# Retnet attention into a SwiGLU block on one core: the last quad of w_out's sums on VectorE, and ScalarE's part of the second tile's ticks at once

## The chip, the cores and the metric

One core of one Trainium2 chip runs the whole program in one launch. The metric is the device time of an execution in microseconds. The kernel before was run four times, and one more execution was profiled.

## What is computed

```python
# q, k, v: (8, 8, 576, 64); w_gate, w_val: (512, 1536); w_out: (1536, 512)
scores = scale * q @ k.T                       # for each batch and head, scale = 1/sqrt(64)
ret    = scores * D                            # D[i, j] = gamma_h ** (i - j) for i >= j, else 0
attn   = ret @ v
x      = attn.transpose(0, 2, 1, 3).reshape(4608, 512)
g      = x @ w_gate
out    = (g * sigmoid(g) * (x @ w_val)) @ w_out
```

All of it is float32.

## The kernel before

**Attention** runs over 32 *items*: 8 batches by 4 pairs of heads (HP = 4), numbered `i`. A pair's 576 tokens are cut into 9 chunks of 64. Within a chunk the masked scores are multiplied out; what earlier chunks give comes from a running state of 64x64 a head. `tick(t)` (L595) advances three items by one stage each: TensorE's values of item t-2 (L481 `own_values`, L500 to L504 `earlier_values`), the new states of item t-1 (L490) and its scores (L511 for the last chunk, L517). The work of the other engines in the tick is a list of *pieces* that `go_on` (L633) issues one or more at a time: `copies` (L528, `even`), `keys` (L459 and the like, the scaling of kn), `outputs` (`to_x`, L554 to L577, which write x), `own` (L524, `ret`), `states` (L532 `ret_last`, L534 to L539 `state`), the transposes of item t to qT and kT (L454), and last the load of item t+2. A load (L258) of an item from 4 on is 13 DMAs: eight of q and k (L291), two of kn and two of v (L272), one of `vl` (L301). They stand on SP's queue, except item 11's, which stand on ScalarE's. There are two buffers for q and k together, so a load waits until the transposes have read the buffer that it overwrites. For items that are `light` (L420, from 12 to 19) `keys`, the scaling of q and `outputs` are ScalarE's; else VectorE does most of it.

**The weights** arrive as bits of 64-bit numbers. `split` (L369, ScalarE, L378 and L379) and `rounding` (L384, VectorE) turn each half into float32; each rounding issues the next split.

**The first tile** of 512 tokens is multiplied plainly: `up0` (L645, L650), `down0` (L660, 12 down products of four matmuls in the order `down_order`), `out0` (L665), which copies the result and issues four output DMAs on ScalarE's queue (L670).

**Every further tile** has 1024 tokens and goes by a bilinear scheme: four by four blocks with 26 products instead of 32, for each of three quads of the up weights (`up_step` L854, matmuls L870, 78 in a tile) and once for all three quads of w_out (`down_step` L900, matmuls L909, 26 in a tile). A product's operands are sums of blocks, and its result is added into several parts (`reads` L797: copies L807 on ScalarE, sums L810 on VectorE or GpSimd). The weights' operands are made once and kept in DRAM: those of the up weights by `first_sums` and `w_sums` (L843, L830) during the second tile's up products, those of w_out by `out_sums` (L702) during the first tile. `fetch` (L766, L771) brings them back on SP's queue into a ring of 8 places, one fetch issued behind each product; the first eight, dn0 to dn7, are issued behind the last four products of the second tile's up phase.

**w_out's sums.** A list `OUT_SUMS` (L106) says, for each of 26 operands, which sums lead to it. `out_sums(qd)` makes nine groups of up to three operands of it for each quad. In `do` (L724) a sum takes the first free place of `sum_places` (six of 128x256, L693; 12 more, L694, from late in the first tile's up products on), and a finished operand is sent to DRAM (L728). A place goes back to the end of the list when its value is used no more; a sum that takes it again waits for the DMA that read it. `add` (L676) issues a sum on a given engine: L686 adds or subtracts, L679 and L684 negate, L681 is VectorE's one-instruction form of a negated sum that GpSimd makes with L683 and L684. Before the change all three quads are GpSimd's, and their DMAs SP's.

**Order.** The order on every engine is written by hand: the program order holds. Startup is L936 to L948; the first tile's up products and ticks 4 to 9 follow a plan (L957 to L986); in the loop L988 to L999 each down product of the first tile is followed by pieces of ticks 10 to 13, by `first_sums` and x's sums at its end, and by one or two of the groups of w_out's sums that are left. L1008 to L1027 are the tiles, in which ticks are spread over the products: `up_step` issues one piece behind each product, `down_step` three.

Of the kernel before, what the change touches and what calls it, by code (L numbers as in the profile page):

```python
# [17 lines left out]
ALU = mybir.AluOpType  # L18
# [136 lines left out]
def kernel(  # L155
# [32 lines left out]
    nc = tc.nc  # L188
# [331 lines left out]
    def masked(i):  # L520
        p, sr, (ret, ret_last, state) = i % HP, last_scores(i), places(i)

        def own():
            nc.vector.tensor_tensor(out=ret, in0=sc, in1=near[:, 2 * p : 2 * p + 2].unsqueeze(2).to_broadcast([P, 2, NFULL, L]),  # L524
                                    op=ALU.mult)

        def copies():
            (nc.vector.tensor_copy if vector(i + 1) else nc.scalar.copy)(out=even, in_=z[:, 0])  # L528

        def states():  # L530

            nc.vector.tensor_tensor(out=ret_last, in0=sr, in1=last_near[:, p], op=ALU.mult)  # L532
            at = state[:, 1:].rearrange("p (c r) d -> p c r d", r=2)[:, :, 1]
            nc.vector.scalar_tensor_tensor(out=at, in0=even, scalar=step[:, p : p + 1], in1=z[:, 1], op0=ALU.mult, op1=ALU.add)  # L534
            for c in range(1, NFULL):
                nc.vector.scalar_tensor_tensor(out=at[:, c], in0=at[:, c - 1], scalar=step[:, HP + p : HP + p + 1],
                                               in1=at[:, c], op0=ALU.mult, op1=ALU.add)
            at = state[:, 0 : NC - 1].rearrange("p (c r) d -> p c r d", r=2)
            nc.vector.scalar_tensor_tensor(out=at[:, :, 1], in0=at[:, :, 0], scalar=step[:, p : p + 1], in1=even,  # L539
                                           op0=ALU.mult, op1=ALU.add)  # L540

        return [copies, own, states]

# [51 lines left out]
    def tick(t, lo=HP, hi=NP, spread=False, then=None):  # L595
        go_on(len(pieces))
        if hi == HP:

            if lo <= t - 1 < hi:
                scores(t - 1, True)  # L600
                new_states(t - 1)
                for f in masked(t - 1):
                    f()
            if lo <= t - 2 < hi:
                own_values(t - 2)
                earlier_values(t - 2)
                to_x(t - 2)[0]()
            for f in transposes(t) if lo <= t < hi else ():
                f()
            return  # L610
        if lo <= t - 2 < hi:
            own_values(t - 2)
        if lo <= t - 1 < hi:
            new_states(t - 1)
        if lo <= t - 2 < hi:
            earlier_values(t - 2)
        if lo <= t - 1 < hi:
            scores(t - 1, t - 2 < lo)
        copies, *masks = masked(t - 1) if lo <= t - 1 < hi else (lambda: None,)
        keys, *new = transposes(t) if lo <= t < hi else (lambda: None,)  # L620
        outputs = to_x(t - 2)[0] if lo <= t - 2 < hi else lambda: None
        if t - 2 >= 0 and light(t - 2):
            pieces.append(lambda: (copies(), keys(), outputs()))
        else:
            pieces.extend([lambda: (copies(), keys()), outputs])
        pieces.extend(masks)
        pieces.extend(new)
        if then:
            pieces.append(then)
        if not spread:  # L630
            go_on(len(pieces))
# [33 lines left out]
    def out0():  # L665
        for i, bank in enumerate(banks):
            o = rest[:, part_at + 512 * i : part_at + 512 * (i + 1)]
            (nc.vector.tensor_copy if i > 1 else nc.scalar.copy)(out=o, in_=bank)
        for i in range(4):
            nc.scalar.dma_start(out=out[i * P : (i + 1) * P, :], in_=rest[:, part_at + 512 * i : part_at + 512 * (i + 1)])  # L670
# [5 lines left out]
    def add(eng, op, view, to=None):  # L676
        dst, srcs = view(int(op[1])) if to is None else to, [view(int(a)) for a in op[2:]]
        if op[0] == "neg":
            eng.tensor_scalar(out=dst, in0=srcs[0], scalar1=-1.0, scalar2=None, op0=ALU.mult)  # L679
        elif op[0] == "nad" and eng is nc.vector:  # L680
            eng.scalar_tensor_tensor(out=dst, in0=srcs[0], scalar=-1.0, in1=srcs[1], op0=ALU.mult, op1=ALU.subtract)  # L681
        elif op[0] == "nad":
            eng.tensor_tensor(out=dst, in0=srcs[0], in1=srcs[1], op=ALU.add)  # L683
            eng.tensor_scalar(out=dst, in0=dst, scalar1=-1.0, scalar2=None, op0=ALU.mult)  # L684
        else:
            eng.tensor_tensor(out=dst, in0=srcs[0], in1=srcs[1], op=ALU.add if op[0] == "add" else ALU.subtract)  # L686
# [3 lines left out]

    sum_places = [rest[:, sum_at + TB * i : sum_at + TB * (i + 1)] for i in range(6)]  # L693
    more_places = [rest[:, raw_at + TB * i : raw_at + TB * (i + 1)] for i in range(16) if i % 4]  # L694

    events = []
    for line in OUT_SUMS:
# [3 lines left out]

    def out_sums(qd):  # L702

        place = {}

        def view(s):
            return w_dn[:, qd, s // 2, s % 2] if s < 8 else place[s]

        def used(e):
            return [e[1]] if e[0] is None else [int(a) for a in e[1][2:]]  # L710

        def release(k):

            for s in list(place):
                for e in events[k + 1 :]:
                    if s in used(e):
                        break
                    if s == e[0]:
                        sum_places.append(place.pop(s))
                        break  # L720
                else:
                    sum_places.append(place.pop(s))

        def do(k):  # L724
            e = events[k]
            if e[0] is None:
                _, slot, i = e
                nc.sync.dma_start(out=dn_ops[i][:, qd * TB : (qd + 1) * TB], in_=view(slot))  # L728
            else:
                new = sum_places.pop(0)  # L730
                add(nc.gpsimd, e[1], view, new)
                if e[0] in place:
                    sum_places.append(place[e[0]])
                place[e[0]] = new
            release(k)

        r, ends = [], [k for k, e in enumerate(events) if e[0] is None]
        for g in range(0, N, 3):
            lo, hi = ends[g - 1] + 1 if g else 0, ends[min(g + 2, N - 1)] + 1

            def group(lo=lo, hi=hi):
                for k in range(lo, hi):
                    do(k)

            r.append(group)
        return r
# [188 lines left out]

    for t in range(HP + 2):  # L936
        tick(t, 0, HP)
        if t == 2:
            split(0)

        for j in {2: (0,), 3: (1, 2), 4: (3, 4, 5)}.get(t, ()):
            rounding(j)
        if t == 3:
            load(HP)
        if t > 3:
            for f in range(2):
                up0(f, range(2) if t == 4 else range(2, HP))
# [6 lines left out]
        if t + AHEAD < NP:  # L954
            load(t + AHEAD)

    groups = [(qd, group) for qd in range(NQ) for group in out_sums(qd)]  # L957
    todo = [m for m in range(3, len(order))]
    plan = []

# [7 lines left out]
    for f in range(2, NF):  # L968
        round_until({4: 12, 6: 13, 8: 14, 9: 15, 10: 16, 11: 17}.get(f, f + 2))
        plan.append(lambda f=f: up0(f, range(HP)))  # L970
        if f - 1 in tick_at and f < NF - 1:
            plan.append(lambda t=tick_at[f - 1]: next_load(t))
        if f in tick_at:
            plan.append(lambda t=tick_at[f]: tick(t, HP, FIRST))
        if f >= NF - 2:

            plan.append(lambda t=tick_at[f]: next_load(t))
        for _ in range(0 if f == 9 else 3):
            if f >= (7, 10, NF)[groups[0][0]]:
                if f + 1 == NF and more_places:  # L980
                    plan.append(lambda places=more_places[:]: sum_places.extend(places))
                    more_places.clear()
                plan.append(lambda group=groups.pop(0)[1]: group())
    assert not todo
# [3 lines left out]
    for m, f in enumerate(down_order):  # L988
        down0(f)
        go_on(4)  # L990
        if m in tick_at:
            tick(tick_at[m], HP, FIRST, tick_at[m] + 1 < needed(1))
            go_on(1)
        if m == 8:
            first_sums(0, 0, 4)
        if m > 8:
            x_sums(1, 3 * (m - 9), min(3 * (m - 8), X_FIRST), True)
        for _ in range(min(1 if m < 3 else 2, len(groups))):
            groups.pop(0)[1]()  # L999
    out0()  # L1000
    x_sums(1, X_FIRST, X_FIRST_OF_ALL, True)
    done = FIRST
# [55 lines left out]
```

## Time and profile before

| | before |
|---|---|
| four runs, us | 1081.28, 1083.24, 1088.47, 1078.66 |
| median, us | 1082.26 |
| profiled execution: its own time, us | 1080.27 |
| profiled execution: span on the core, us | 1078.6 |
| mean granted clock of TensorE | 0.989 |
| DVE busy in the span, us | 652.8 |
| POOL busy in the span, us | 414.4 |

Times in the trace count from the span's start. PE is TensorE, PEld its weight loads, DVE VectorE, ACT ScalarE, POOL GpSimd, SP SyncE; ACTq and SPq are the DMA issues on those engines' queues. In the timeline a row gives the start, the time from the first start to the last end of a run of like instructions, the engine, the line, the operation with its tiles (output <- inputs), how many there are, and in brackets the idle time of the engine before it with what ended it. In the list of waits a row gives the instruction that waited, what it waited for, us in total, how many times, and the longest. The granted clock is the share of full speed that TensorE was given.

The places that the change touches lie thus in the trace before: startup until 33 us, the first tile's up products until 128, its down products from 131.3 to 183.7 with ticks 10 to 13 at 138.4, 148.2, 161.4 and 171.2, the second tile's up products from 183.66 and its down products from 355.56.

### The profile page before, as it was taken

How to read it: one execution, taken by the hardware profiler on the slowest of the kernel's cores; microseconds unless marked ns; L12 is line 12 of the kernel's file. 1: busy time of each engine (PE TensorE's matmuls, PEld its weight loads, DVE VectorE, ACT ScalarE, POOL GpSimd, SP SyncE). 2: the span in 40 equal slices, each digit the busy share in tenths (PEclk: the TensorE clock that was granted, in tenths of full speed). 3: DMA queues.
4: the chain of work that ended last, by engine and by line, in shares of the span. 5: the costliest groups of instructions: out<-in, count | busy, mean ns of one | idle time of the engine just before them, and what ended most of it. 6: DMA issues, size and time to landing. Idle time of an engine off the chain costs nothing.

```text
span 1078.6 us, 21481 instructions
## 1 busy us (share of the span) xinstructions
PE 1042.8 (97%) x8420; PEld 855.1 (79%) x8420; DVE 652.8 (61%) x1069; ACT 271.6 (25%) x578; POOL 414.4 (38%) x372
## 2 busy tenths in 40 slices
PE   5999999699999999999999999999999999999998
PEld 4545555488788788888888888888888888888887
DVE  3568755577878857753647868536267455244644
ACT  3456400124333211222222112132221012231110
POOL 5002449666464403741216025622150374122505
PEclk9899999699999999999999999999999999999999
DMA  9798774766586868767657778554454555555653
GB/s 246 220 273 233 214 176 151 215 183 187 160 211 182 253 154 244 216 179 198 157 160 219 179 206 229 151 153 137 154 174 152 160 179 150 155 152 157 187 160 98
DMA packets 300700, 198.58 MB, mean 184 GB/s; under 512 B 215352, under 2 KB 244056, under 8 KB 300600
## 3 DMA queue, kind: packets, MB, share of 16 engines
q1 hardware_dynamic: 268230, 159.16, 54.2%
q10 hardware_dynamic: 31954, 37.17, 10.3%
q8 instruction: 67, 1.10, 0.4%
q0 software_dynamic: 416, 0.89, 0.2%
q14 instruction: 33, 0.27, 0.1%
HBM read 157.04 MB, written 40.11 MB: 183 GB/s over the span
## 4 chain that ended last, share of the span: by engine, by line
PE 80%; DVE 6%; POOL 5%; DMA 4%; issue 2%; SPq 1%; ACT 1%; ACTq 0%; DVEq 0%; POOLq 0%
PE bankC L870 11%; PE bankA L870 11%; PE bankB L870 11%; PE bankE L870 11%; PE bankA L909 6%; PE bankE L909 6%; PE bankB L909 6%; PE bankC L909 6%; POOL rest L686 3%; DVE rest L810 2%; PE bankA L650 2%; PE bankC L650 2%; PE bankB L650 2%; PE bankE L650 2%; PE outer L504 2%
## 5 line engine op out<-in xcount | busy, mean ns | idle before, releaser
L810 POOL TENSOR_TENSOR rest<-rest 128x512 f32<-128x512 f32 x56 | 79.2, 1419 | 298.6 <-DVE rest L810 278.0
L885 ACT ACTIVATE io<-rest 128x256 f32<-128x256 f32 x180 | 75.0, 417 | 342.9 <-DVE rest L810 296.4
L870 PE MATMUL bankA<-rest,arena 128*128 128x256 f32 x544 | 130.8, 384 | 4.5 <-ACT rest L807 3.6
L870 PE MATMUL bankC<-rest,arena 128*128 128x256 f32 x544 | 129.1, 380 | 0.5 <-DVE rest L810 0.5
L686 POOL TENSOR_TENSOR arena<-arena 128x512 f32<-128x512 f32 (+1 forms) x72 | 115.2, 1612 | 27.9 <-DMA up<-arena 20.1
L870 PE MATMUL bankE<-rest,arena 128*128 128x256 f32 x512 | 122.4, 382 | 0.8 <-DVE rest L810 0.8
L870 PE MATMUL bankB<-rest,arena 128*128 128x256 f32 x512 | 121.4, 380 | 0.4 <-DVE rest L810 0.4
L686 POOL TENSOR_TENSOR rest<-rest 128x256 f32<-128x256 f32 (+1 forms) x86 | 80.5, 958 | 105.7 <-issue 63.2
L870 PEld LDWEIGHTS bankA<-rest,arena 128*128 128x128 f32 x544 | 103.9, 192 | 20.7 <-issue 5.6
L892 POOL TENSOR_TENSOR arena<-rest,io 128x256 f32<-128x256 f32 x72 | 51.8, 726 | 167.1 <-ACT io L885 167.1
L870 PEld LDWEIGHTS bankC<-rest,arena 128*128 128x128 f32 x544 | 102.9, 190 | 15.3 <-issue 1.2
L870 PEld LDWEIGHTS bankE<-rest,arena 128*128 128x128 f32 x512 | 97.8, 192 | 14.8 <-issue 1.2
L870 PEld LDWEIGHTS bankB<-rest,arena 128*128 128x128 f32 x512 | 97.0, 190 | 14.3 <-DVE rest L810 0.8
L810 DVE TENSOR_TENSOR rest<-bankB,rest 128x512 f32<-128x512 f32 x72 | 48.9, 687 | 65.0 <-PE bankB L870 47.0
L810 DVE TENSOR_TENSOR rest<-bankE,rest 128x512 f32<-128x512 f32 x72 | 48.8, 686 | 64.3 <-PE bankE L870 45.8
L810 DVE TENSOR_TENSOR rest<-bankC,rest 128x512 f32<-128x512 f32 x72 | 48.8, 686 | 63.3 <-PE bankC L870 43.7
L810 DVE TENSOR_TENSOR rest<-bankA,rest 128x512 f32<-128x512 f32 x72 | 48.8, 685 | 61.4 <-PE bankA L870 43.0
L888 DVE SCALAR_TENSOR_TENSOR arena<-rest,io 128x256 f32<-128x256 f32 x84 | 58.7, 703 | 11.7 <-ACT io L885 11.7
L909 PE MATMUL bankA<-arena 128*128 128x256 f32 x252 | 58.0, 380 | 1.3 <-DVE arena L686 1.3
L909 PE MATMUL bankB<-arena 128*128 128x256 f32 x252 | 58.3, 381 | 0.0
L909 PE MATMUL bankC<-arena 128*128 128x256 f32 x252 | 58.1, 380 | 0.0
L909 PE MATMUL bankE<-arena 128*128 128x256 f32 x252 | 57.9, 379 | 0.0
(179 smaller groups left out, 1632.0 us busy)
## 6 DMA issues: line engine op xcount, KB each, us to landing
arena<-up SPq DMA_DIRECT2D x234, 256.0 KB
arena<-dn SPq DMA_DIRECT2D x104, 384.0 KB
up<-arena ACTq DMA_DIRECT2D x78, 256.0 KB
dn<-rest SPq DMA_DIRECT2D x78, 128.0 KB
out_dram<-rest SPq DMA_DIRECT2D x32, 256.0 KB
qk<-in_q_dram SPq DMA_DIRECT2D x108, 72.0 KB
qk<-in_k_dram SPq DMA_DIRECT2D x108, 72.0 KB
v<-in_v_dram SPq DMA_DIRECT2D x58, 128.0 KB
```

Of the source, the lines that this page charges most:

```text
L504: nc.tensor.matmul(xr[half[hl]] if c + 1 == NC else xo[half[hl ^ c % 2 * exchange(i)], c // 2, c % 2], state[half[hl], c, :], s["qT"][half ...
L650: nc.tensor.matmul(bank, w_up[:, f // 4, gv, f % 4, c // 2, (c % 2) * P : (c % 2 + 1) * P], xs[0][:, c, :], start=(c == 0), stop=(c == HP ...
L686: eng.tensor_tensor(out=dst, in0=srcs[0], in1=srcs[1], op=ALU.add if op[0] == "add" else ALU.subtract)
L810: eng.tensor_tensor(out=at(op[1]), in0=at(op[2]), in1=at(op[3]), op=ALU.add if op[0] == "add" else ALU.subtract)
L870: nc.tensor.matmul(b[:, gv * TB : (gv + 1) * TB], w[:, gv, ts(c, P)], rhs[:, c, :], start=(opens and gv == 0 and c == 0), stop=(c == 1), s ...
L885: nc.scalar.activation(out=s, in_=src[:, 0:TB], func=AF.Silu, scale=-1.0 if negative else 1.0)
L888: return lambda: nc.vector.scalar_tensor_tensor(out=dst, in0=src[:, TB : 2 * TB], scalar=-1.0, in1=s, op0=ALU.mult, op1=ALU.mult)
L892: nc.gpsimd.tensor_tensor(out=dst, in0=src[:, TB : 2 * TB], in1=s, op=ALU.mult)
L909: nc.tensor.matmul(b[:, m * TB : (m + 1) * TB], lhs[:, qd, ts(m, P)], w[:, qd], start=(opens and qd == 0 and m == 0), stop=(qd == NQ - 1), ...
```

## The change

It has three parts.

1. *Startup:* `split(0)` and `rounding(0)` are issued within tick 3, behind item 2's masks and states, instead of after tick 2.
2. *w_out's last quad:* its sums are made by VectorE instead of GpSimd, its DMAs go on ScalarE's queue instead of SP's, and it has six sum places of its own (`more_places[6:]`); GpSimd has 12 instead of 18. Its nine groups are issued one behind each of the first tile's down products from the first on; GpSimd's remaining groups of the second quad also come one at a time. Of the 27 instructions that GpSimd spent on it VectorE needs 24.
3. *Ticks that write outputs of `light` items:* `copies`, `keys` and `outputs` are issued in the tick itself instead of as the first piece, so that all later pieces, the load among them, come one product earlier. In the same ticks `ret_last` comes after the states.

TensorE's order is unchanged. On SP's queue the load of the tick that lies at the end of the second tile's up products comes ahead of the fetches dn0, dn1 and dn2; it came between dn2 and dn3 before.

```diff
         def copies():
             (nc.vector.tensor_copy if vector(i + 1) else nc.scalar.copy)(out=even, in_=z[:, 0])
 
+        def last():
+            nc.vector.tensor_tensor(out=ret_last, in0=sr, in1=last_near[:, p], op=ALU.mult)
+
+
+        wait = i > 0 and light(i - 1)
+
         def states():
-
-            nc.vector.tensor_tensor(out=ret_last, in0=sr, in1=last_near[:, p], op=ALU.mult)
+            if not wait:
+                last()
+
             at = state[:, 1:].rearrange("p (c r) d -> p c r d", r=2)[:, :, 1]
...
                                            op0=ALU.mult, op1=ALU.add)
+            if wait:
+                last()
 
         return [copies, own, states]
...
                 for f in masked(t - 1):
                     f()
+            if t == 3:
+                split(0)
+                rounding(0)
             if lo <= t - 2 < hi:
...
         if t - 2 >= 0 and light(t - 2):
-            pieces.append(lambda: (copies(), keys(), outputs()))
+
+            copies()
+            keys()
+            outputs()
         else:
...
-    sum_places = [rest[:, sum_at + TB * i : sum_at + TB * (i + 1)] for i in range(6)]
+    pool_places = [rest[:, sum_at + TB * i : sum_at + TB * (i + 1)] for i in range(6)]
     more_places = [rest[:, raw_at + TB * i : raw_at + TB * (i + 1)] for i in range(16) if i % 4]
+    vector_places = more_places[6:]
...
     def out_sums(qd):
 
+
         place = {}
+        eng, queue, sum_places = ((nc.vector, nc.scalar, vector_places) if qd + 1 == NQ else (nc.gpsimd, nc.sync, pool_places))
...
-                nc.sync.dma_start(out=dn_ops[i][:, qd * TB : (qd + 1) * TB], in_=view(slot))
+                queue.dma_start(out=dn_ops[i][:, qd * TB : (qd + 1) * TB], in_=view(slot))
             else:
                 new = sum_places.pop(0)
-                add(nc.gpsimd, e[1], view, new)
+                add(eng, e[1], view, new)
...
     for t in range(HP + 2):
         tick(t, 0, HP)
-        if t == 2:
-            split(0)
-
-        for j in {2: (0,), 3: (1, 2), 4: (3, 4, 5)}.get(t, ()):
+
+        for j in {3: (1, 2), 4: (3, 4, 5)}.get(t, ()):
             rounding(j)
...
-    groups = [(qd, group) for qd in range(NQ) for group in out_sums(qd)]
+    groups = [(qd, group) for qd in range(NQ - 1) for group in out_sums(qd)]
+    last_groups = out_sums(NQ - 1)
...
-                    plan.append(lambda places=more_places[:]: sum_places.extend(places))
+                    plan.append(lambda places=more_places[:6]: pool_places.extend(places))
                     more_places.clear()
...
-        for _ in range(min(1 if m < 3 else 2, len(groups))):
+        if groups:
             groups.pop(0)[1]()
+        if last_groups:
+            last_groups.pop(0)()
     out0()
```

## The prediction

> **What bounds the kernel now.** I read the page, then what TensorE waited for, then the timeline at each place that the change touches. Busy time, slices and granted clock:
>
> ```profile
> span 1078.6 us, 21481 instructions
> PE 1042.8 (97%) x8420; PEld 855.1 (79%) x8420; DVE 652.8 (61%) x1069; ACT 271.6 (25%) x578; POOL 414.4 (38%) x372
> PE   5999999699999999999999999999999999999998
> POOL 5002449666464403741216025622150374122505
> PEclk9899999699999999999999999999999999999999
> ```
>
> TensorE is busy 97%, at full clock except in slices 2 and 8 (27 to 54 and 189 to 216 us). So nothing is won but in a hole of TensorE, and any new hole costs in full. The waits of TensorE that this change can touch:
>
> ```profile
> PE bankC L870 <- POOL arena L686: 8.1, 1, 8.1
> PE bankA L870 <- ACT rest L807: 3.6, 1, 3.6
> PE bankE L511 <- DVE state L534: 3.1, 1, 3.1
> PE bankB L909 <- DMA arena<-dn: 1.4, 1, 1.4
> ```
>
> The first two are one place, the start of the first 1024-token tile (timeline, 190 to 212 us):
>
> ```profile
> 190.37 3.68 POOL L686 TENSOR_TENSOR rest<-rest 128x256 f32<-128x256 f32 x5
> 194.01 2.93 POOL L686 TENSOR_TENSOR arena<-arena 128x512 f32<-128x512 f32 x2
> 195.32 3.78 PE L870 MATMUL bankC<-x_odd,arena 128*128 128x256 f32 x8 [8.05 <-POOL arena L686]
> 195.85 7.19 ACTq L670 DMA_DIRECT2D out_dram<-rest  x4
> 205.44 3.75 PE L870 MATMUL bankA<-rest,arena 128*128 128x256 f32 x8 [3.62 <-ACT rest L807]
> 211.82 1.89 PE L870 MATMUL bankE<-rest,arena 128*128 128x256 f32 x8
> ```
>
> GpSimd does w_out's last quad until 194.0 and only then the arena sums that product 3 reads. The second hole is a ScalarE copy behind the four output DMAs of L670. After each hole 8 matmuls take 3.75 us instead of 1.89, and the granted clock is 0.56 from 195.3 to 201.8 and from 205.4 to 212.0. Two products (16 matmuls, full pace 3.46) take 6.70 after the first hole: **half clock costs 3.2 us per hole**. [...]
>
> The other two places, tick 11 beside the first tile's down products, and the end of the second tile's up products:
>
> ```profile
> 146.77 1.10 ACTq L301 DMA_DIRECT2D vl<-in_v_dram  x1
> 148.17 0.69 PE L481 MATMUL outer<-ret,v 64*64 64x64 f32 x32
> 149.30 0.74 DVE L454 STREAM_TRANSPOSE kT<-qk 128x576 f32<-128x576 f32 x1
> 151.31 1.46 POOL L686 TENSOR_TENSOR rest<-rest 128x256 f32<-128x256 f32 x2 [13.19 <-DMA dn<-rest]
> 346.43 8.24 SPq L771 DMA_DIRECT2D arena<-dn  x3
> 354.77 3.13 SPq L291 DMA_DIRECT2D qk<-in_q_dram  x4
> 355.56 2.75 PE L909 MATMUL bankA<-arena 128*128 128x256 f32 x12
> 364.06 4.46 SPq L771 DMA_DIRECT2D arena<-dn  x8
> 367.81 0.45 PE L909 MATMUL bankB<-arena,rest 128*128 128x256 f32 x1 [1.39 <-DMA arena<-dn]
> ```
>
> To see here: sums reuse their places only after the place's DMA (GpSimd stood 13.19 us for one), and SP issues three dn fetches, then a load of 13 DMAs until 363.97, then dn3, which TensorE waits for.
>
> **The change part by part** (against the profiled execution, 1080.27 us of its own, span 1078.6; the runs' median, 1082.26, lies 2.0 above).
>
> *Startup.* The split and rounding of w_gate's first piece go behind item 2's copy (ScalarE 25.81, 0.36) and VectorE's ret and state (26.94). The 3.14 us wait of L511 ends on that state. But L511 also needs ScalarE's kT copy, which ends at 27.37: the weight rounding stays ahead of it, and it moves up only by the copy's slot (25.81 to 26.06), 0.25. With the 0.20 that L481 waits at 29.62 for VectorE: **-0.45** (0 if the weights land as late anyway; -1 if the load behind gains too).
>
> *The last quad on VectorE.* It leaves GpSimd 18 sum places less 6 (12), and 24 VectorE instructions come in, one group behind each down product of the first tile. GpSimd loses the 27 instructions that kept it until 194.0 (some 22 us at the row's 0.73), so it is through at about 170 and the arena sums are done by 183. Product 3 then follows product 2 at full pace, and the 26 last-quad DMAs are no longer on SP behind which places come late. Without any new wait product 7 starts at 183.66 + 6 x 1.73 = 194 to 196 instead of 211.8 to 213.5: -16 to -17.7. ScalarE's copy behind L670's DMAs may keep some of it; at 1.73 a product it has 5 us more.
>
> The new wait: VectorE has only 6 places. Group 0 takes four; group 1's third sum (sub 11 11 8) takes the place of dn14, the first that came free, and must wait for dn14's DMA. That DMA now stands on ScalarE's queue behind item 11's 13 loads, which end with vl (146.77 + 1.10 = 147.9; 148.4 if the queue waits for kn to land). A 128 KB dn DMA takes 2.75 to land there (148.43 to 151.18): VectorE stands from 146.0 to about 151. Queued behind: the outputs of item 8, ret and ret_last (146.73 before, then 153.4), the state, qT, four more sums at 0.4 to 0.8 and kT, 149.30 before, then 158.3 to 160. TensorE waits at L481 (148.17 to 153.6) and at L511 (150.2 to 160): 8 to 10 us late together, and with 1.6 to 3.2 of half clock **+12** (8 to 14). Ticks 12 and 13 have room: VectorE idled 6.55 and 4.44 there, and kT would come at 172 where TensorE asks at 175.7, so a margin of 3.8. Tile 1 then starts at 196 and product 7 at 208 against 213.5: **-5.4** in all (-10 to -3.5; -16 with no stall).
>
> What a sum costs VectorE is 0.41 (128x256, L568's row) to 0.89 (L891, GpSimd busy); L686's own 128x512 takes 0.68 alone and 1.10 to 1.22 with GpSimd adding (174.3 to 183). I take 0.41 to 0.8. [...]
>
> *ScalarE's part at once, in the second tile.* Copy, keys and outputs are issued at the tick, so the VectorE pieces come one product earlier, ret_last after the states. VectorE is full there (19.21 of 20 us busy at 280 to 300, 19.43 at 340 to 360), and its stalls are small: 0.3 to 0.8 each, 1.32 at 393. The same work in another order: **+0.5** (-2 if the stalls close; +3 if four of them grow by 0.8).
>
> *SP's order.* One piece earlier also moves a load's 13 DMAs. At the border to the down products they now stand ahead of dn0 to dn2. The load waits for kT (351.22 before, 0.76 long; about 350.7 now) and takes 9.2 us (354.77 to 363.97; other loads 7.5 to 11.8). dn0 is then issued at 360 instead of 346.43 and lands 3.75 later (dn3: 364.06 to 367.81): L909 starts at 363.7 instead of 355.56, +8.2; with 3.2 of half clock, less the 1.39 for dn3 that goes away, **+9.8** (+4, if the load starts early and takes 7.5; +12). The load's early landing helps nobody: it was hidden.
>
> Sum: -0.45 - 5.4 + 0.5 + 9.8 = +4.4, so 1080.27 + 4.4 = **1084.7; I say 1085**. About 1% is what a measurement of this kernel can tell from no change.
>
> **The rivals.** *R1, no wait at tick 11.* If dn14 lands before VectorE asks for its place (146), the quad brings -16 and the total is 1084.7 - 10.6 = 1074.1. For it: DMAs of one queue may overlap, and dn14's data are ready at 142. Against: GpSimd's 13.19 us wait for the same kind of DMA. *R2, the load does not hold dn0.* 1084.7 - 9.8 = 1074.9. [...] *R1 and R2 together:* 1064. *R3, slower.* The sums cost VectorE over 1.1 us each beside GpSimd's, nine of them in the stretch before tick 12: from 0.7 to 1.1 eats the margin of 3.8, beyond it tick 12 has a hole like tick 11's, 5.7 + 3.2 = +8.9: 1093.6. For it: 1.10 to 1.22, up to 1.75, on L686; against: those are twice as wide. *R4, the gain does not come:* product 7 still waits for the copy behind L670's DMAs, 3.62 + 3.2 = +6.8 on the main case, 1091.5.
>
> **How the numbers follow.** Chances: the main case 0.45, R1 0.18, R2 0.14, both 0.08, R3 0.09, R4 0.06. The main case's own range is 1077 to 1091 (its bounds on the quad and on SP's order, -4.6 to +1.9 and -5.8 to +2.2, with startup and ticks). The range, leaving out both-together and the upper end of R3 with the tails of R1, R2: 1069 to 1094. Faster than 1071.4: both, and a third of R1 and R2, 0.2. Slower than 1093.1: half of R3, a third of R4, a tenth of the main case, and what I can't see, 0.16. The rest 0.64.
>
> **What would show it.** Right: no wait of L870 for POOL at tile 1 and products 1.73 apart from 184 on; a VectorE idle of some 5 us near 146 ended by a dn DMA, with L511 late by 8 to 10; L909's first product waiting 8 us for arena<-dn with granted clock near 0.56 after it; L511 at 27 us nearly where it was. Wrong: dn14 landed early (R1), SP's load rows ending before 355 (R2), sums over 1.1 us (R3), a copy L807 still behind L670 (R4). If the ticks of the second tile open holes that are now 0.3 to 0.8, the third term is wrong.

## The result, and the profile after

The changed kernel takes 1085.71 us in the median of 36 runs (1081.89 to 1089.06), the kernel before 1081.95 in the median of 55: a ratio of 1.0037, 95% interval [1.0025, 1.0048]. So it is about 4 us slower, 2.7 to 5.2 by the interval. The profiled execution took 1084.64 of its own, span 1082.9, against 1080.27 and 1078.6.

Read it as before, the page first (busy time of each engine, slices of the span, granted clock):

```profile
span 1082.9 us, 21463 instructions
PE 1042.0 (96%) x8420; PEld 855.2 (79%) x8420; DVE 663.3 (61%) x1093; ACT 272.8 (25%) x578; POOL 393.6 (36%) x345
PE   5999969999899699999999999999999999999998
POOL 5002454465454302741215025622151375122505
PEclk9999989999999899999999999999999999999999
```

POOL has lost 20.8 us and DVE has gained 10.5: the quad is on VectorE. TensorE's thin slices have moved. The one at 189 to 216 us is full, and there is one at 135 to 162 (a 6) and one at 352 to 379 (a 6). The list of TensorE's waits says what they are (instruction, what it waited for, us in total, times, longest):

```profile
PE bankA L927 <- DVE arena L696: 8.2, 1, 8.2
PE outer L481 <- DVE ret_last L531: 6.1, 1, 6.1
PE bankE L511 <- ACT kT L444: 4.3, 3, 2.8
PE bankA L888 <- DVE rest L828: 3.1, 2, 2.7
PE bankE L888 <- DVE rest L828: 2.6, 1, 2.6
PE outer L511 <- DVE kT L454: 2.3, 1, 2.3
```

Line numbers of the new kernel are shifted: L870 is now L888, L909 L927, L810 L828, L686 L701, L532 L531, L771 L789. The waits for GpSimd (8.1) and for ScalarE's copy (3.6) at the second tile's start are gone, and these have come. (The third stands mostly at startup, where TensorE waited 3.1 for VectorE's state before.)

Tick 11 in the timeline of the changed kernel:

```profile
145.36 17.53 ACTq L746 DMA_DIRECT2D dn<-rest  x10
149.85 0.86 DVE L701 TENSOR_TENSOR rest<-rest 128x256 f32<-128x256 f32 x1 [4.19 <-DMA dn<-rest]
152.42 1.13 PE L481 MATMUL outer<-ret,v 64*64 64x64 f32 x32 [6.12 <-DVE ret_last L531]
155.18 2.98 DVE L701 TENSOR_TENSOR rest<-rest 128x256 f32<-128x256 f32 x4
158.08 0.77 DVE L454 STREAM_TRANSPOSE kT<-qk 128x576 f32<-128x576 f32 x1
158.90 0.27 PE L511 MATMUL outer<-qT,kT 64*64 64x64 f32 x2 [2.31 <-DVE kT L454]
```

VectorE stands 4.19 us for a dn DMA before it may write a sum; ret_last, four sums and kT queue behind, and TensorE waits twice.

The start of the second tile (product 1 at 194.93, product 3 at 198.38, product 7 at 205.28):

```profile
193.54 2.64 ACTq L685 DMA_DIRECT2D out_dram<-rest  x4
194.93 1.89 PE L888 MATMUL bankA<-rest,arena 128*128 128x256 f32 x8
198.38 1.89 PE L888 MATMUL bankC<-x_odd,arena 128*128 128x256 f32 x8
205.28 1.89 PE L888 MATMUL bankE<-rest,arena 128*128 128x256 f32 x8
```

The tile starts 11.3 us later than before (183.66) and stands 6.5 us ahead at product 7 (211.82 before). GpSimd, which worked on w_out's sums until 194.0 before, has nothing to do from 172.9 to 186.4. The border to the down products:

```profile
345.79 0.76 DVE L454 STREAM_TRANSPOSE kT<-qk 128x576 f32<-128x576 f32 x1
346.62 1.96 SPq L291 DMA_DIRECT2D qk<-in_q_dram  x4
356.59 0.54 SPq L301 DMA_DIRECT2D vl<-in_v_dram  x1
357.24 11.62 SPq L789 DMA_DIRECT2D arena<-dn  x10
361.42 4.49 PE L927 MATMUL bankA<-arena 128*128 128x256 f32 x12 [8.23 <-DVE arena L696]
365.75 2.75 PE L927 MATMUL bankB<-arena 128*128 128x256 f32 x12
```

The load's 13 DMAs occupy SP's queue from 346.62 to 357.13; only then is dn0 issued, 4.2 us before TensorE starts.

Where the time went is seen best by setting the same TensorE work side by side. This table is worked out from the timelines: the start of L481 in a tick, minus that of before (negative: ahead). The rows of the experiments are used below.

| profiled execution | tick 10 (138.4 before) | tick 12 (161.4) | tick 14 (278.2) | tick 17 (334.7) | tick 18 (360.8) | from tick 20 on |
|---|---|---|---|---|---|---|
| changed kernel | -1.9 | +10.4 | -6.0 | -4.6 | +7.6 | +4.4 |
| startup_alone | -2.1 | -1.1 | -2.9 | -3.6 | -3.9 | -1.6 |
| quad_alone | -2.8 | +8.8 | -6.3 | -6.4 | -6.6 | -7.6 |
| ticks_alone | -2.3 | -2.3 | -2.9 | -0.4 | +11.4 | +8.2 |
| load_behind | -0.4 | +11.0 | -3.0 | -0.2 | +1.9 | -1.3 |
| ten_places | -2.7 | +0.6 | -16.6 | -15.4 | -3.3 | -6.5 |
| both_mended | +1.0 | +7.1 | -10.4 | -9.0 | -6.7 | -9.9 |
| no_ticks_ten | -3.1 | +3.8 | -13.2 | -13.5 | -13.8 | -14.7 |
| quad_ten | +2.1 | +6.5 | -10.2 | -10.6 | -10.6 | -10.3 |
| keys_first | -1.0 | +0.7 | -15.6 | -15.9 | -16.3 | -15.9 |
| at_once_only | -0.5 | +1.6 | -14.4 | -13.4 | -12.9 | -11.9 |
| load11_sp | -1.5 | +7.3 | -9.4 | -7.7 | +2.8 | -0.4 |

Three things happen: 12.3 us are lost at tick 11, 16.4 are won at the second tile's start, and 12.2 are lost between ticks 17 and 18, of which 3.2 come back by tick 20. From tick 20 on nothing changes by over 0.1. A row is one execution, and executions of one kernel differ by 5 us or more (before: 1076.4 to 1088.47), so differences *within* a row are the safer ones, and sizes are given by the runs' ratios where there are any.

### The profile page after: what moved, and what is told of

The parts are those of the page before. It is cut to its first block, busy times and chain, and to the rows that moved or that the text cites. A ratio compares the mean times of both kernels' runs of the same rounds, so it can differ in the third digit from the quotient of the medians.

```text
span 1082.9 us, 21463 instructions
## 1 busy us (share of the span) xinstructions
PE 1042.0 (96%) x8420; PEld 855.2 (79%) x8420; DVE 663.3 (61%) x1093; ACT 272.8 (25%) x578; POOL 393.6 (36%) x345
## 4 chain that ended last, share of the span: by engine, by line
PE 85%; DVE 8%; DMA 4%; issue 1%; POOL 1%; SPq 1%; ACT 1%; ACTq 0%; DVEq 0%; POOLq 0%
PE bankC L888 11%; PE bankE L888 11%; PE bankA L888 11%; PE bankB L888 11%; PE bankA L927 6%; PE bankB L927 6%; PE bankC L927 6%; PE bankE L927 6%; DVE rest L828 3%; PE bankA L665 2%; PE bankC L665 2%; PE bankE L665 2%; PE bankB L665 2%; PE outer L504 2%; PE outer L481 2%
## 5 line engine op out<-in xcount | busy, mean ns | idle before, releaser
L828 POOL TENSOR_TENSOR rest<-rest 128x512 f32<-128x512 f32 x56 | 79.1, 1419 | 306.9 <-DVE rest L828 288.4
L888 PE MATMUL bankA<-rest,arena 128*128 128x256 f32 x544 | 130.5, 383 | 3.1 <-DVE rest L828 3.1
L701 POOL TENSOR_TENSOR arena<-arena 128x512 f32<-128x512 f32 (+1 forms) x72 | 114.6, 1604 | 42.5 <-DMA up<-arena 22.3
L888 PE MATMUL bankC<-rest,arena 128*128 128x256 f32 x544 | 129.1, 380 | 0.5 <-DVE rest L828 0.5
L888 PE MATMUL bankE<-rest,arena 128*128 128x256 f32 x512 | 121.4, 380 | 2.6 <-DVE rest L828 2.6
L888 PE MATMUL bankB<-rest,arena 128*128 128x256 f32 x512 | 121.5, 380 | 1.0 <-POOL arena L857 0.6
L888 PEld LDWEIGHTS bankA<-rest,arena 128*128 128x128 f32 x544 | 104.0, 192 | 18.8 <-issue 3.5
L888 PEld LDWEIGHTS bankC<-rest,arena 128*128 128x128 f32 x544 | 102.9, 190 | 15.3 <-issue 0.9
L888 PEld LDWEIGHTS bankE<-rest,arena 128*128 128x128 f32 x512 | 96.9, 190 | 16.6 <-issue 2.9
L888 PEld LDWEIGHTS bankB<-rest,arena 128*128 128x128 f32 x512 | 96.9, 190 | 15.2 <-POOL arena L857 1.3
L701 POOL TENSOR_TENSOR rest<-rest 128x256 f32<-128x256 f32 (+1 forms) x66 | 65.6, 1015 | 103.1 <-issue 61.1
L828 DVE TENSOR_TENSOR rest<-bankE,rest 128x512 f32<-128x512 f32 x72 | 48.9, 686 | 67.4 <-PE bankE L888 49.1
L828 DVE TENSOR_TENSOR rest<-bankC,rest 128x512 f32<-128x512 f32 x72 | 48.9, 687 | 66.2 <-PE bankC L888 46.0
L828 DVE TENSOR_TENSOR rest<-bankB,rest 128x512 f32<-128x512 f32 x72 | 48.8, 686 | 65.3 <-PE bankB L888 47.3
L828 DVE TENSOR_TENSOR rest<-bankA,rest 128x512 f32<-128x512 f32 x72 | 48.9, 687 | 62.7 <-PE bankA L888 45.4
L927 PE MATMUL bankA<-arena 128*128 128x256 f32 x252 | 59.7, 388 | 8.2 <-DVE arena L696 8.2
L906 DVE SCALAR_TENSOR_TENSOR arena<-rest,io 128x256 f32<-128x256 f32 x84 | 55.4, 664 | 11.1 <-ACT io L903 11.1
L927 PEld LDWEIGHTS bankA<-arena 128*128 128x128 f32 x252 | 48.9, 195 | 15.5 <-issue 8.6
L927 PE MATMUL bankB<-arena 128*128 128x256 f32 x252 | 58.3, 381 | 0.0
L927 PE MATMUL bankC<-arena 128*128 128x256 f32 x252 | 58.1, 380 | 0.0
```

The source lines that it names most:

```text
L828: eng.tensor_tensor(out=at(op[1]), in0=at(op[2]), in1=at(op[3]), op=ALU.add if op[0] == "add" else ALU.subtract)
L888: nc.tensor.matmul(b[:, gv * TB : (gv + 1) * TB], w[:, gv, ts(c, P)], rhs[:, c, :], start=(opens and gv == 0 and c == 0), stop=(c == 1), s ...
L906: return lambda: nc.vector.scalar_tensor_tensor(out=dst, in0=src[:, TB : 2 * TB], scalar=-1.0, in1=s, op0=ALU.mult, op1=ALU.mult)
L927: nc.tensor.matmul(b[:, m * TB : (m + 1) * TB], lhs[:, qd, ts(m, P)], w[:, qd], start=(opens and qd == 0 and m == 0), stop=(qd == NQ - 1), ...
```

## The experiments

The theory is that of the prediction: two orders make the loss (dn14's place on VectorE at tick 11, the load ahead of dn0 on SP's queue), and GpSimd's freed time makes the gain. The rivals were that the hole at the border comes from VectorE's sum L696, which the list of waits names; that tick 11 suffers from the number of sums and not from the place; and that one part alone does it all.

### Each part by itself

The startup part alone:

```diff
+            if t == 3:
+                split(0)
+                rounding(0)
...
-        if t == 2:
-            split(0)
```

> The kernel before with the startup part alone. In the profile of the changed kernel TensorE is 1.9 us ahead from 40 us on. Theory 1: the gain reaches the end, 1.9 us faster than before. Theory 2: it ends at the first hole of the second tile, which GpSimd's last quad sets and not TensorE: then TensorE is 1.9 us ahead until 183 and the hole there is as much longer, and the time is that of before within 0.5 us, unless GpSimd's sums also start earlier.

Measured: 1077.53 against 1079.56, ratio 0.9985 [0.9971, 0.9999]: 0.1 to 3.1 us faster. In the profile the hole at the second tile is still there, L873 waits 7.0 for POOL (8.1 before) and 4.3 for ScalarE (3.6), and TensorE's lead is 1.1 at tick 12, 2.9 at tick 14 and 1.6 at the end. Neither theory is excluded by this alone.

The quad alone (`eng, queue, sum_places` by quad, and the groups one behind each down product):

```diff
+        eng, queue, sum_places = ((nc.vector, nc.scalar, vector_places) if qd + 1 == NQ else (nc.gpsimd, nc.sync, pool_places))
```

> The kernel before with the last quad's sums on VectorE alone. Theory 1 (the sum of the prediction): tick 11 comes out 12 us late through dn14's place, the holes at the second tile's start (some 17 us) go, 4 to 6 us faster than before. Theory 2: the tick's lateness is that of another cause (the ticks' new order); then no wait of VectorE for a dn DMA near 146 us, and 16 us faster.

Measured: 1073.78, ratio 0.9963 [0.9940, 0.9985], 4.0 us faster (1.6 to 6.5). Theory 1. The waits of TensorE and the row of VectorE in the timeline of this kernel:

```profile
PE outer L481 <- DVE ret_last L532: 6.1, 2, 5.3
PE outer L511 <- DVE kT L454: 2.3, 1, 2.3
148.43 0.68 DVE L686 TENSOR_TENSOR rest<-rest 128x256 f32<-128x256 f32 x1 [4.38 <-DMA dn<-rest]
```

The place is waited for without the ticks' part, and the row of the table loses 11.6 between ticks 10 and 12 and wins 15.1 by tick 14. This part moves the sums and their DMAs at once, so that GpSimd's freed time, and not the DMAs gone from SP's queue, makes the gain is argued from the traces (in the changed kernel GpSimd is through at 172.9 instead of 194.0) and not shown by an edit of its own.

The ticks alone (ScalarE's part at once, ret_last last):

```diff
-            pieces.append(lambda: (copies(), keys(), outputs()))
+            copies()
+            keys()
+            outputs()
```

> The kernel before with the ticks of the second tile alone (ScalarE's part at once, ret_last after the states, all pieces one product earlier). Theory 1: the load ahead of dn0 opens a hole of 6 to 8 us at the first down product of the second tile, with 1.7 us of half clock, and VectorE's states ahead of its reads of the banks open one or two holes of 2 to 3 us in the up products: 8 to 12 us slower than before. Theory 2: the hole at the down products comes from the rest of the change (a DVE sum that the trace names): then within 3 us of before.

Measured: 1090.35, ratio 1.0112 [1.0090, 1.0134], 12.1 us slower (9.7 to 14.5). Theory 1, at its upper end. Its waits name the DMA, where those of the changed kernel name a sum:

```profile
PE bankA L918 <- DMA arena<-dn: 8.0, 1, 8.0
PE bankA L879 <- DVE rest L819: 3.1, 2, 2.7
PE bankE L879 <- DVE rest L819: 2.6, 1, 2.6
```

The three parts give -1.6, -4.0 and +12.1 by their ratios: +6.5 together, against +4.0 [2.7, 5.2] measured, within what the intervals allow. The ticks' part is what made the kernel slower.

### The load on SP's queue

An empty piece ahead of the load, in the second tile's ticks:

```diff
             outputs()
+            if then:
+                new.append(lambda: None)
```

> The changed kernel with an empty piece ahead of the load in the second tile's ticks, so that each load comes one product later and the one at the border stands behind dn2, as before. Theory 1 (SP's order makes the hole): L927's first product waits under 1 us, the later wait for dn3 comes back (about 1.4), and the time is 8 to 9 us below the changed kernel's, 4 to 5 below that of before. Theory 2 (VectorE's sum L696, which the list of waits names): the hole of 8 us stays.

Measured: 1074.24, ratio 0.9942 [0.9919, 0.9964] to before. Against the changed kernel's 1.0037 that is 0.9905, 10 us below it (7 to 13, from the two intervals). SP's queue and the first down products in its timeline:

```profile
342.20 13.38 SPq L791 DMA_DIRECT2D arena<-dn  x3
355.69 2.97 SPq L291 DMA_DIRECT2D qk<-in_q_dram  x4
357.43 2.75 PE L929 MATMUL bankA<-arena 128*128 128x256 f32 x12
360.02 2.75 PE L929 MATMUL bankB<-arena 128*128 128x256 f32 x12
363.29 2.56 DVE L698 SCALAR_TENSOR_TENSOR arena<-arena 128x768 f32<-128x768 f32 x1
```

dn0 is issued at 342.20, the wait is gone and so is the half clock: 2.75 for 12 matmuls instead of 4.49. The sum L696 (L698 here) is still in the kernel, in the same place of VectorE's order, and it now runs from 363.29 to 365.85, when TensorE has long begun. So the first down product does not need it; in the changed kernel it only ended at the instant, 358.87 + 2.55 = 361.42. One expectation missed: the wait for dn3 of about 1.4 did not come back.

### The place of dn14

Ten places for VectorE, eight for GpSimd:

```diff
-                    plan.append(lambda places=more_places[:6]: pool_places.extend(places))
+                    plan.append(lambda places=more_places[:2]: pool_places.extend(places))
...
-    vector_places = more_places[6:]
+    vector_places = more_places[2:]
```

> The changed kernel with ten sum places for VectorE and eight for GpSimd (six and twelve). Theory 1 (the place of dn14 is what VectorE waits for): VectorE's wait of 4.2 us for a dn DMA near 146 goes, L481's 6.1 and most of L511's 2.3 with the half clock after them too, and the time is 10 to 12 us below the changed kernel's. Theory 2 (nine more VectorE instructions among the tick's, each up to 0.9): L481 and L511 stay late by over half, and the time falls by under 5. A third possibility: GpSimd with eight places falls behind and the hole at the second tile's start is back.

Measured: 1078.35, ratio 0.9983 [0.9963, 1.0003]; against the changed kernel 0.9946, 5.8 us below it (3 to 8). In the profile no VectorE instruction waits for a dn DMA any more and L481's 6.1 is gone, but L511 waits longer:

```profile
PE bankA L927 <- DMA arena<-dn: 7.9, 1, 7.9
PE outer L511 <- DVE kT L454: 3.0, 1, 3.0
146.18 0.77 DVE L454 STREAM_TRANSPOSE qT<-qk 128x576 f32<-128x576 f32 x1
146.87 3.11 DVE L701 TENSOR_TENSOR rest<-rest 128x256 f32<-128x256 f32 x4
149.91 0.77 DVE L454 STREAM_TRANSPOSE kT<-qk 128x576 f32<-128x576 f32 x1
```

The place made L481 late (theory 1); what is left at L511 is the four sums between qT and kT, so theory 2 holds for that part. GpSimd with eight places is not too late. The gain by the runs is half of what was expected. The profiled execution, 10.9 us below the changed kernel's, was the fastest of the twelve (1073.75 to 1082.20), and in it kn landed early (VectorE's keys at 141.12 instead of 143.83), so its own gain is not to be taken for the size.

Item 11's load on SP instead of ScalarE, with six places:

```diff
-            queues = (nc.scalar, nc.scalar)
+            queues = (nc.sync, nc.sync)
```

> The changed kernel with item 11's load on SP's queue instead of ScalarE's, six places. Theory 1 (dn14's DMA is late because it stands behind that load): VectorE's wait for the place, 4.2 us, falls under 1 us, and with it L481's 6.1; the time falls by 4 to 8 unless the load itself comes later on SP, which the transpose qT would show. Theory 2 (the DMA takes that long whatever stands ahead, some 4 us from issue to landing): the wait stays at 3 to 4 us.

Measured: 1080.78, ratio 1.0009 [0.9992, 1.0026]; against the changed kernel 0.9972, 3 us below it (1 to 5). Its timeline:

```profile
137.63 24.46 ACTq L746 DMA_DIRECT2D dn<-rest  x9
146.02 0.35 DVE L459 TENSOR_SCALAR kn<-kn,tab 128x256 f32<-128x256 f32 x1 [5.87 <-DMA kn<-in_k_dram]
147.26 0.75 DVE L701 TENSOR_TENSOR rest<-rest 128x256 f32<-128x256 f32 x2
149.73 1.13 PE L481 MATMUL outer<-ret,v 64*64 64x64 f32 x32 [3.01 <-DVE ret_last L531]
```

The dn DMAs in the row are issued from 137.63 on, and not only from 145.36, and VectorE's wait for the place is gone: the load ahead on ScalarE's queue was what made dn14 late. But kn now lands later (VectorE waits 5.87 for it, 4.10 in the changed kernel), so half of L481's wait stays, below the 4 to 8 expected. Two cures of one place, one by more places and one by its queue, both remove VectorE's wait.

### Both mendings, and the kernel without the ticks

> The changed kernel with both mendings: ten places, and the load one product later. Theory 1: the two add up, about 20 us below the changed kernel's, 1064 to 1066. Otherwise a hole opens elsewhere, first at the second tile's start.

Ten places and the empty piece together: 1069.11, ratio 0.9890 [0.9870, 0.9911], 16 us below the changed kernel by the ratios (13 to 18), the sum of 10 and 5.8. So the two costs add up, within the intervals; the 20 that were expected counted ten places too high.

> The kernel before with the startup and the quad's part, ten places for VectorE, and none of the ticks' part. Theory 1: 1.9 us from the startup and 16 to 17 from the holes, so 1063 to 1065, and if VectorE's states ahead of its bank reads cost 2 to 4 us in the second tile this one is 1 to 4 us faster than the one with both mendings. If the ticks' part is worth something by itself, this one is the slower.

Startup and quad with ten places, none of the ticks' part: 1066.80, ratio 0.9867 [0.9845, 0.9888]. This is faster by 2.3 in the medians than with the mended ticks; the intervals overlap, but the profile of the mended one has the holes and this one has not: L890 waits 2.6 and 3.0 for VectorE's L830 there, and the longest wait for such a read here is 0.8. It stays 1.8 above the range that was expected; L511 still waits 3.1 for kT at tick 11.

> The kernel before with the quad's part and ten places, without the startup and the ticks' part. Two profiles without the startup part already have TensorE 2.3 and 2.8 us ahead of before at 40 us, so the 1.9 of the changed kernel's profile may be chance. Theory 1 (the startup part is worth its 1.5 to 2 us): 1.5 to 2 above the kernel with startup, quad and ten places (1066.8). Theory 2 (it is chance): the same within 1 us.

The same without the startup part: 1068.33, ratio 0.9882 [0.9859, 0.9905]. The 1.5 between the medians goes the way of startup_alone, but the intervals overlap widely, and neither theory is settled.

### The rest of tick 11, and of the ticks

kT ahead of the sums:

```diff
         down0(f)
-        go_on(4)
+        go_on(5)
```

> Startup, quad and ten places without the ticks' part, and five pieces behind a down product of the first tile where there were four, so that kT's transpose stands ahead of the four sums and not behind them. Theory 1 (the sums stand between qT and kT and TensorE waits for kT): L511's 3.1 us at tick 11 goes, and the time is 3 to 4.5 below that kernel's 1066.8. Theory 2: the sums come late instead, and the wait turns up at the next tick or at the second tile's start: no gain.

Measured: 1062.11, ratio 0.9839 [0.9814, 0.9863], 4.7 us below the kernel without this edit in the medians, 3 by the ratios, whose intervals overlap. That the wait goes is seen in the trace, at tick 11:

```profile
150.09 0.73 DVE L454 STREAM_TRANSPOSE kT<-qk 128x576 f32<-128x576 f32 x1
150.75 2.25 DVE L689 TENSOR_TENSOR rest<-rest 128x256 f32<-128x256 f32 x4
150.88 0.27 PE L511 MATMUL outer<-qT,kT 64*64 64x64 f32 x2 [0.20 <-DVE kT L454]
```

L511 waits 0.20. In the table the loss between ticks 10 and 12 is 1.7, where it was 6.9 without the edit and 12.3 in the changed kernel. This version lies 17 us (15 to 20) below the kernel before and 21 below the changed one.

> The kernel with kT ahead of the sums, and of the ticks' part only this: copies, keys and outputs are issued at the tick (with an empty first piece, so that VectorE's pieces and the load stay where they were) and ret_last after the states. Theory 1 (what cost 2.3 us beside the load is that VectorE's pieces come one product earlier): no holes of 2.6 and 2.7 us in the second tile's up products, and the time is that of the kernel with kT ahead, within 1 us. Theory 2 (issuing ScalarE's part at once, or ret_last, is what costs): those two holes are there and it is 2 to 4 us slower.

The same kernel with ScalarE's part at once and ret_last last, but VectorE's pieces and the load where they were (an empty first piece):

```diff
+            copies()
+            keys()
+            outputs()
+            pieces.append(lambda: None)
```

Measured: 1064.31, ratio 0.9850 [0.9825, 0.9876]. The holes of 2.6 and 2.7 are 1.03 and 1.04, without half clock (8 matmuls in 1.99 us). So most of each hole comes from VectorE's pieces one product earlier. The time is 2.2 above that of the kernel with kT ahead in the medians, where within 1 was expected; whether the rest of the part costs that is not settled, since the intervals overlap.

## Why the prediction came out

The total was right, and the mechanisms are the ones named. That the profiled execution came out at 1084.64 against a forecast of 1084.7 is in part luck: executions of one kernel differ by 5 us and more, and errors inside the terms cancelled. By the runs' ratio the change costs 4.0 (2.7 to 5.2). Within the profile the two halves fit: startup and quad -6.0 at tick 14 (-5.85 forecast), ticks and SP's order +10.4 behind it (+10.3). Step by step:

- **Startup (-0.45).** The releaser was right: L511 now waits 2.75 for ScalarE's kT, instead of 3.14 for VectorE's state. The size stays open. The changed kernel's profile is 1.9 ahead there, but so are profiles of kernels without the edit (quad_alone 2.8, ticks_alone 2.3; quad_ten is 2.1 behind), and one with it is 1.0 behind (both_mended). By runs the part is worth 0.1 to 3.1.
- **The quad (-5.4).** Right in each link, by the timeline of tick 11: VectorE held 4.19 (5 forecast), kT at 158.08 (158.3 to 160), TensorE's waits 6.12 + 2.31 = 8.4 (8 to 10), late by 12.3 with the half clock (12), the tile started at 194.93 (196). The 1.6 at the low end of that half clock was an estimate that no run shows: beyond the 8.4 of waits tick 11 lost 3.9, at a granted clock of 0.68 from 152.4 to 159. Inside the first link two errors cancelled: the first dn DMA was issued at 145.36 and not at 148.4, and VectorE went on 4.5 after that and not 2.75. Net -4.1 in the changed kernel's profile, -4.0 in quad_alone's runs.
- **Two readings in that sum.** The forecast's 208 and 213.5 are called product 7 but belong to product 8 (196 + 7 x 1.73; before, product 7 starts at 211.82 and product 8 at 213.54). The difference holds, since both are one product late; product 8 came at 207.01, ahead by the 1.1 of the tile's start. Half clock after a hole was put at 3.2 (6.70 for two products); the rows of before give 2.9: product 7 starts 6.38 after the product at 205.44 instead of 3.45.
- **The price of the place.** What the place alone costs is less than the whole stall: R1, without the wait at tick 11, was priced 10.6 below the main case, and mending the place gives 5.8 back. kT ahead of the sums gives about 3 more, and its wait goes in the trace. The one stall had two causes, and the prediction had both in its sum but put the whole to the place.
- **The ticks (+0.5).** This is the mis-sized term. "0.3 to 0.8 each" were taken to stay about that size; two became 2.58 and 2.70, because six VectorE instructions of the states now stand ahead of the read that frees the bank (at_once_only moves them back, and 1.03 and 1.04 are left). The three L543 at 339.94 alone took 2.33, and 0.93 at 347.52 before; GpSimd added beside them now (337.69 to 341.86) and stood idle then (345.21 to 352.41), but whether that is the reason was not tested. The part without the load costs 2.3 between the medians of both_mended and no_ticks_ten, whose intervals overlap.
- **SP's order (+9.8).** Right: 8.23 of wait (8.2 forecast) and 1.74 of half clock, not 3.2; 10 by the runs of load_behind. Seen from TensorE, which came to the border at 353.19 (355.56 forecast), three errors cancelled: the load began 6.6 ahead of it instead of 4.9 (346.62; 350.7 forecast), took 10.5 instead of 9.2, and dn0 was there 4.2 after its issue instead of 3.75.
- **The rivals.** R1 and R2 did not come. R3: from tick 11 to tick 12 the sums took 0.38 to 0.95, four in 2.98, so tick 12 kept its margin (+10.4 at tick 12, +10.5 at tick 13); one later sum took 1.49 (at 171.72). R4: the copy waited 2.86 for an output DMA and TensorE did not wait for it.

So the gain of the change did come, 16.4 us at the second tile's start, and was given back at two places where the same change altered what stands ahead in a queue.

## What to carry to other kernels

When work moves to another engine, list what its instructions and its DMAs now stand behind and ahead of on every queue: here the gain of 16 us was lost to one DMA behind a load on ScalarE's queue, four sums ahead of a transpose, and one load ahead of three fetches on SP's. A load issued earlier is a loss when it was hidden anyway and its queue holds something that was not (here 8.23 us of wait). To find such a place, compare the start of the same TensorE work in the two traces and look only where the difference jumps; a releaser that the list of waits names is a suspect until an edit takes it away.

## What the runs showed of the hardware

How much a hole costs beyond itself was not fixed by its length. The same hole of 2.58 us, ended by the same VectorE read, was followed by 8 matmuls in 1.97 us in the changed kernel (granted clock 1.00 in the 6.8 us after it) and by 8 in 3.50 in ticks_alone (0.76). These are the rows of the two timelines:

```profile
287.22 1.97 PE L888 MATMUL bankE<-rest,arena 128*128 128x256 f32 x8 [2.58 <-DVE rest L828]
290.47 3.50 PE L879 MATMUL bankE<-rest,arena 128*128 128x256 f32 x8 [2.58 <-DVE rest L819]
```

Other holes of 2.5 to 3.1 us were followed by slow matmuls too: 2.49 in at_once_only (12 matmuls in 4.30 instead of 2.75), 2.57 and 2.71 in load_behind (8 in 3.54 and 3.62), 2.70 in ticks_alone (8 in 3.45, granted 0.77) and in the changed kernel (8 in 3.60, granted 0.75), and 3.05 in both_mended (8 in 3.55). But 2.58 in both_mended and 2.71 in load11_sp were followed by full pace (8 in 1.97). After single holes of 1.03 to 1.93 in front of up and down products the timelines show full pace each time (8 in 1.97 to 1.99, 12 in 2.83 to 2.86). The extra cost seen is 0 to 1.8 us for holes of 2.5 to 2.7, 1.74 for 8.23, 2.4 for 6.83 in load11_sp, and 2.9 for the 8.05 and 3.62 before.
